# True phase and sizes of PE's instruction blocks in a hand-made list; ut by eight PE transposes; join, nb and y in two pieces

## The chip, the cores and the metric

One core of one Trainium2 chip. The time is device microseconds of one execution of the whole program; the figure is the median of three runs of the kernel.

## The reference

Three parts follow each other: a recurrence over 768 time steps in 32 heads of 40 x 40 state, an MLP of 320 to 2048 to 320, and a gated MLP of 320 to 1536 to 320, both over 3072 tokens.

```python
for t in range(S):                                     # B, H, S, D = 4, 8, 768, 40
    y[:, :, t] = einsum('bhd,bhde->bhe', rt, state)
    Sa = einsum('bhde,bhe->bhd', state, at)
    state = state * wt[:, :, None, :] - einsum('bhd,bhe->bhde', Sa, bt)
    state = state + einsum('bhd,bhe->bhde', vt, kt)
x = y.transpose(0, 2, 1, 3).reshape(B * S, H * D)      # 3072 x 320
h = x @ w_in;  x = (h * sigmoid(1.702 * h)) @ w_out
g = x @ w_gate
return (g * sigmoid(g) * (x @ w_val)) @ w_out2
```

## The kernel before

**Stages.** The recurrence is worked in 12 steps (NT) of 64 time points (T). Step n has two halves: `prepare` (line 637: decay scans, the products nb and nk of the scaled a, b, k, and a triangular solve that gives tt) and `advance` (line 952: w, u, ut, the state update m, the scores sv and su, and the output y, which `give` splits in two and puts into the rows xst of the first MLP). Two steps make one group of 512 tokens for the first MLP (`Up`), whose pieces (`h_part` line 460, `o_part` line 497, eight matmuls each of 512 columns) are called dense here; the attention's matmuls have 32 to 64 columns and are called thin. The gated MLP (`Down`) comes last and is written out by itself.

**The order of the work.** Attention, dense pieces and the weights' conversion are tasks of one `Plan` (line 72). `Plan.order` (line 123) deals them once, when the program is built, into one list; each engine then runs its part of the list in that order, and real waits are kept by semaphores. The dealer keeps a clock of its own: a task has an engine, a cost in us, a due time, and on PE two more things.

- *Density.* Ahead of a thin task it puts up to four dummy matmuls (`warm`, line 435, printed as line 437) until a sum of column work over the last 3.4 us reaches 4000 (lines 199 to 205). It also fills with dummies where PE would sit idle, up to the first dense piece and wherever the dense pieces' one PSUM bank is free (line 195). A dummy writes that bank, from an operand of zeros, `still`.
- *Blocks.* It counts PE instructions (`count`, line 112, 2 to 4 for a matmul with its loads) in `sent`, from 0, and takes it that a block of 256 can't begin earlier than 3.8 us (FETCH) after the one ahead. `cross` adds the missing time to a task, line 185 prefers a dense piece where a thin one would run through a block too fast, and lines 206 to 211 put dummies ahead of a task that would have to wait for a block.

The size of a task in instructions is guessed from its cost: 128 below 1.7 us, 256 below 3 us, 16 for dense pieces and what is shorter than 1.05 us.

**What the change touches.** In `prepare`: `nb_mm` (line 710, 64 matmuls in one task), and in the solve of the first five steps (`pieces`, line 770) `cross_mm` (line 840) and `join_mm` (line 853, 64 matmuls). In `advance`: `u_mm` and its copy `u_out` by ACT into u, a tile of 16 x 40; `ut_mm` (line 1007), which makes u transposed by 32 thin fp32 matmuls (64 matmul records) from w and tt; `m_one` (line 1039), `m_two` (line 1050); the `scores` (line 1151), where ut's halves stand crossed for four of eight heads (`odd`); and `y_one` (line 1115), which in one task adds the old state's part (`y_state`, 32 fp32 matmuls with a drain) and the first half of the new part (`y_part`).

Of the kernel before, what the change touches and what calls it, by code (L numbers as in the profile page):

```python
# [51 lines left out]
class Task:  # L52
    def __init__(self, n, eng, cost, fn, deps, due, bank, kb, same, port):
        self.n, self.fn, self.due, self.deps, self.bank, self.kb, self.same = n, fn, due, deps, bank, kb, same
        self.port = port
        self.choice = dict(zip(eng, cost)) if isinstance(eng, tuple) else {eng: cost}
# [15 lines left out]
class Plan:  # L72
# [5 lines left out]
    BLOCK, FETCH, PACE, AHEAD = 256, 3.8, 0.5, 0.5  # L78
# [9 lines left out]
    def add(self, eng, cost, fn, reads=(), writes=(), due=0.0, after=(), bank=None, kb=0, into=(), same=None, port=True, work=None):  # L88
# [11 lines left out]
        t.work = work  # L100
# [22 lines left out]
    def order(self):  # L123
# [3 lines left out]
        wire = port = hold = began = 0.0  # L127
        sent, pe = 0, []
# [25 lines left out]
        def cross(k, now, cost):  # L154
            nonlocal sent, began
            stop, left = 0.0, self.BLOCK - sent % self.BLOCK
            if k >= left:
                x = now + cost * left / k
                stop = max(0.0, began + self.FETCH - x)
                began = x + stop  # L160
            sent += k
            return stop

        def filler(t, now):
            w = self.fill(t, now)
            w.end += cross(2, now, w.end - now)
# [7 lines left out]
        while True:  # L174
# [17 lines left out]
            if e == "PE":  # L192
# [4 lines left out]
                if t.due < 1e6 and hold < 1e8:  # L197
# [14 lines left out]
                stop = cross(k, now, t.choice[e])  # L212
# [158 lines left out]
class Up:  # L371
# [9 lines left out]
    def __init__(self, tc, ctx, keep, cst, w_out, x2s, side):  # L381
# [13 lines left out]
        self.still = k.tile([128, 128], F32R, name="still")  # L395
# [161 lines left out]
class Attention:  # L557
    EARLY = 5


    def __init__(self, tc, ctx, cst, src, up):
# [21 lines left out]
        self.ut = one.tile([104, 2, H, T], F32, name="ut")  # L583
# [10 lines left out]
        self.u = one.tile([128, 16, D], F32, name="u")  # L594
# [20 lines left out]
        v.memset(self.cend, 1.0)  # L615
        nc.gpsimd.memset(self.mt, 0.0)
# [20 lines left out]
    def prepare(self, plan, n, due):  # L637
# [72 lines left out]
        def nb_mm():  # L710
            ps = self.ps[b.slot]
            x = kb[:, 1]
            for k in range(8):
# [14 lines left out]
        plan.add("PE", 2.4, nb_mm, (ak, "kb1"), ("nb.p",), due + 0.15, bank=b, into=(nbk,), work=1760)  # L728
# [41 lines left out]
        def pieces():  # L770
# [64 lines left out]
            def corners():  # L835
                for i in range(16):
# [16 lines left out]
            def join_mm():  # L853
                ps = self.ps[bt.slot]
                for i, o, c in corners():
# [96 lines left out]
    def advance(self, plan, n, due):  # L952
# [33 lines left out]
        if n:  # L986
            seen = plan.add("PE", 1.2, w_two, (ak, "mt"), ("w.p",), due, bank=bw)
# [12 lines left out]
        def u_out(e):  # L1000
            self.copy(e, self.u.rearrange("q (r k) d -> q r (k d)", r=2), self.ps[bu.slot][:, :, 0:8 * D])
# [19 lines left out]

        def ut_out(e):
            self.copy(e, self.ut.rearrange("q p h t -> q (p h t)"),
# [26 lines left out]
        def m_two():  # L1050
            m_part(1, self.u)
# [18 lines left out]
        if n + 1 < NT:  # L1070
            plan.add("PE", 2.6 if 0 < n < self.EARLY else 1.25, m_one, ("v", "tok0", "mt"), ("m.p",), due + 0.005, bank=bm,
                     work=4300 if 0 < n < self.EARLY else 2200, after=(middle,))
# [6 lines left out]
        plan.add("PE", 1.25, ut_mm, ("w",) + tt, ("ut.p",), due + 0.03, bank=bx, into=("ut",))  # L1079
        plan.add(("ACT",), (1.05,), ut_out, ("ut.p",), ("ut",), due + 0.03, bank=bx)  # L1080

        for src, dst, keys, d in ((self.vt, self.sv, ("vt", "sv"), -0.2), (self.ut, self.su, ("ut", "su"), 0.04)):
            marks = self.scores(plan, src, dst, keys, due + d, src is self.ut)
# [41 lines left out]
        def y_out():  # L1125
# [4 lines left out]
        plan.add("PE", 2.5 if n else 1.25, y_one, ("md", "r", "tok0", "sv"), ("y.p",), due + 0.045, bank=by,  # L1130
                 work=4300 if n else 2500, after=(marks,))
# [19 lines left out]
    def scores(self, plan, src, dst, keys, due, odd):  # L1151
        nc, b = self.nc, self.bank()

        def mm():
            ps = self.ps[b.slot]
            for h in range(H):
                for p in range(2):
                    for z in range(2):
                        d, q = slice(64 * z, 64 * z + D), p ^ h // 4 if odd else p
# [618 lines left out]
```

## Time and profile before

| | |
|---|---|
| median of 3 runs | 1143.59 us (1138.55 to 1144.63) |
| the profiled execution | 1140.57 us, its span 1138.8 us |
| PE busy | 1094.7 us, 96% |
| DVE, ACT, POOL busy | 698.1, 438.1, 108.8 us |
| mean granted clock of PE | 0.978 |

Busy PE time is that of its matmuls, whose ends are modelled; weight loads run beside them and have a row of their own (PEld). [...] A wait that ends on "issue" is one for which the profile shows no other engine and no DMA.

### The profile page before, as it was taken

What the parts mean: (1) busy time and instruction counts of PE and PEld (TensorE: products, weight loads), DVE (VectorE), ACT (ScalarE), POOL (GpSimd) and SP (SyncE); (2) the same over time, 40 slices, a digit from 0 to 9 for tenths busy, and PEclk for the clock granted to TensorE, in tenths of its full rate; (3) what the DMA queues carried; (4) which work ended last, traced back from release to release, by engine and by line L of the source; (5) the groups of instructions that cost most, each with busy time, mean ns of one, the idle gap of its engine ahead of it and who ended that gap; (6) DMA issues with size and microseconds to landing.
All of it is one profiled execution on the core that took longest, in us unless ns stands there. A gap on an engine that the chain in (4) does not pass through costs nothing.

```text
span 1138.8 us, 39991 instructions
## 1 busy us (share of the span) xinstructions
PE 1094.7 (96%) x17403; PEld 908.4 (80%) x17403; DVE 698.1 (61%) x1461; ACT 438.1 (38%) x809; POOL 108.8 (10%) x124
## 2 busy tenths in 40 slices
PE   9888999989999899999999989999999999999987
PEld 7667777767788777877788768788888888888877
DVE  7875788855968687787966166676344344434321
ACT  2434466543434343434335355545222222222221
POOL 1111223301010000000000022221000000000000
PEclk9898999999999999999899999999999999999999
DMA  7245457552534343443423265744233434343000
GB/s 217 88 154 166 149 165 226 159 177 73 180 103 151 112 137 117 134 150 91 145 64 112 83 204 161 218 122 111 75 106 99 129 103 144 93 127 91 24 1 27
DMA packets 141018, 141.99 MB, mean 125 GB/s; under 512 B 16032, under 2 KB 131744, under 8 KB 140832
## 3 DMA queue, kind: packets, MB, share of 16 engines
q1 hardware_dynamic: 134784, 131.48, 38.6%
q10 hardware_dynamic: 6048, 7.86, 2.1%
q8 instruction: 138, 2.26, 0.8%
q14 instruction: 48, 0.39, 0.1%
HBM read 118.04 MB, written 13.11 MB: 115 GB/s over the span
## 4 chain that ended last, share of the span: by engine, by line
PE 84%; DVE 6%; issue 3%; DMA 3%; SPq 2%; ACT 1%; POOL 0%; ACTq 0%; DVEq 0%; POOLq 0%
PE gv L1392 23%; PE h L479 13%; PE sums L511 4%; PE h L437 4%; PE oacc L1413 4%; PE oacc L1412 4%; PE oacc L1411 4%; PE sums L512 3%; PE sums L513 3%; PE ps L1110 2%; PE ps L1034 2%; PE ps L1160 2%; PE sums L507 2%; PE sums L506 2%; PE ps L885 1%
## 5 line engine op out<-in xcount | busy, mean ns | idle before, releaser
L1392 PE MATMUL gv<-xst,wg 128*128 128x512 f32 x1152 | 274.7, 391 | 0.0
L1392 PEld LDWEIGHTS gv<-xst,wg 128*128 128x128 f32 x1152 | 213.8, 188 | 41.3
L479 PE MATMUL h<-xst,wi 120*128 120x512 f32 x768 | 201.8, 405 | 0.4 <-ACT sg L487 0.3
L479 PEld LDWEIGHTS h<-xst,wi 120*128 120x128 f32 x768 | 142.0, 191 | 33.4 <-ACT sg L487 1.6
L1397 DVE TENSOR_TENSOR sg<-gv,sg 128x512 f32<-128x512 f32 x72 | 49.8, 691 | 169.9 <-PE gv L1392 169.2
L487 ACT ACTIVATE sg<-h 128x512 f32<-128x512 f32 x96 | 57.2, 596 | 174.7 <-PE h L479 162.9
L494 DVE TENSOR_TENSOR gl<-sg,gh 128x512 fp32r<-128x512 f32 x82 | 57.5, 701 | 81.7 <-ACT gh L493 81.7
L1398 ACT ACTIVATE gh<-sg 128x512 fp32r<-128x512 f32 x72 | 45.5, 632 | 137.1 <-DVE sg L1397 137.1
L307 POOL TENSOR_TENSOR cvw<-cvu,cva 128x256 uint32<-128x256 uint32 (+2 forms) x89 | 70.9, 798 | 251.1 <-DVE cvu L299 117.9
L1396 ACT ACTIVATE sg<-gv 128x512 f32<-128x512 f32 x72 | 42.9, 596 | 129.1 <-PE gv L1392 128.4
L1413 PE MATMUL oacc<-wo,gl 128*128 128x320 f32 x288 | 89.6, 311 | 0.0
L1412 PE MATMUL oacc<-wo,gh 128*128 128x320 f32 x288 | 89.4, 310 | 0.0
L1411 PE MATMUL oacc<-wo,gh 128*128 128x320 f32 x288 | 89.2, 310 | 0.0
L511 PE MATMUL sums<-gh,wo 128*128 128x512 f32 x192 | 82.0, 427 | 5.8 <-DVE sg L541 4.6
L1399 DVE TENSOR_TENSOR gl<-sg,gh 128x512 fp32r<-128x512 f32 x72 | 49.8, 692 | 50.3 <-ACT gh L1398 50.3
L512 PE MATMUL sums<-gh,wo 128*128 128x512 f32 x192 | 76.5, 399 | 0.0
L513 PE MATMUL sums<-gl,wo 128*128 128x512 f32 x192 | 76.1, 396 | 0.0
L437 PE MATMUL h<-still 128*128 128x512 f32 x232 | 71.4, 456 | 2.0 <-DVE still L396 1.2
L752 DVE TENSOR_TENSOR tsol<-tsol,tmp 128x126 f32<-128x126 f32 (+22 forms) x217 | 58.3, 269 | 6.7
L493 ACT ACTIVATE gh<-sg 128x512 fp32r<-128x512 f32 x96 | 60.7, 632 | 3.5
L744 DVE TENSOR_TENSOR tmp<-tsol,nsol 128x126 f32<-128x126 f32 (+22 forms) x217 | 56.9, 262 | 6.7
L437 PEld LDWEIGHTS h<-still 128*128 128x128 f32 x232 | 47.8, 217 | 12.9 <-DVE still L396 1.2
(176 smaller groups left out, 1652.9 us busy)
## 6 DMA issues: line engine op xcount, KB each, us to landing
wo<-w_out SPq DMA_DIRECT2D x192, 160.0 KB
cva<-out SPq DMA_DIRECT2D x128, 128.0 KB
cva<-gv SPq DMA_DIRECT2D x96, 128.0 KB
kb<-kba SPq DMA_DIRECT2D x92, 104.0 KB
cva<-in_ab SPq DMA_DIRECT2D x64, 120.0 KB
r<-rT SPq DMA_DIRECT2D x48, 104.0 KB
vt<-vT SPq DMA_DIRECT2D x48, 104.0 KB
a<-kba SPq DMA_DIRECT2D x46, 104.0 KB
```

What stands on the lines that cost most here:

```text
L307: nc.gpsimd.tensor_tensor(w.bitcast(U32), u, lo, op=ALU.add)
L437: self.nc.tensor.matmul(self.ph[0].rearrange("q (k c) -> q k c", k=4), c, c.unsqueeze(1).to_broadcast([128, 4, 128]), start=True, stop=True)
L479: nc.tensor.matmul(ps[:, 0:n], self.wi[:, b, 128 * f:128 * f + 128], x[:, a], start=(e == 0), stop=(e == 7))
L493: add("ACT", 0.63, lambda: nc.scalar.activation(out=hi, in_=sg, func=ACTF.Copy), (f"sg{s}",), (f"gh{d}",))
L511: nc.tensor.matmul(acc[k], w[:, c:c + 128], hi, start=st, stop=False)
L512: nc.tensor.matmul(acc[k], w[:, 256 + c:384 + c], hi, start=False, stop=False)
L513: nc.tensor.matmul(acc[k], w[:, c:c + 128], lo, start=False, stop=sp)
L752: self.engine(e).tensor_tensor(t, t, self.tmp[:, 0:(16 - o) * u].rearrange("q (c i) -> q c i", c=16 - o), op=ALU.add)
L1392: nc.tensor.matmul(ps, w[:, b], x[:, a], start=(i == 0), stop=(i == 7))
L1411: nc.tensor.matmul(acc[k], hi[:, c], self.wo[:, f, 0], start=st, stop=False)
L1412: nc.tensor.matmul(acc[k], hi[:, c], self.wo[:, f, 1], start=False, stop=False)
L1413: nc.tensor.matmul(acc[k], lo[:, c], self.wo[:, f, 0], start=False, stop=sp)
```

## The change

- The dealer's block count starts at 63 (HEAD), and tasks may say their size in instructions: nb 256, cross 261, the merged m_one 137, the second half of w and the old part of y 129; ut falls to 16. A dense piece still counts 16.
- A block is taken to need 3.4 us instead of 3.8, and the time that is left in it is reckoned from the matmuls' bare durations (`real`, `least`) plus half (SURE) of what else passed, no longer from the time passed alone.
- nb of step zero (HALVES = 1) and join of the first five steps (EARLY) become two tasks each; the old state's part of y becomes a task `y_old` of its own from step 1 on.
- ut is made from u by eight transposes of 128 x 128 (u is widened to 16 x 64, zeroed once on POOL), laid out by head first, so `odd` goes.
- The dummy's operand `still` becomes one column that is read with step zero, for the weights and for the 512 columns.
- The flag at the end of attention is worked in columns of the tile `good` instead of a tile of its own.

```diff
-    BLOCK, FETCH, PACE, AHEAD = 256, 3.8, 0.5, 0.5
+    BLOCK, FETCH, PACE, AHEAD, HEAD, SURE = 256, 3.4, 0.5, 0.5, 63, 0.5
...
+        return t.size or (16 if t.due >= 1e6 or t.choice["PE"] < 1.05 else 128)
+
+    def least(self, t):
+
         c = t.choice["PE"]
-        return 16 if t.due >= 1e6 or c < 1.05 else 128 if c < 1.7 else 256 if c < 3 else 384
+        return t.real or (1.87 if t.due >= 1e6 else min(c, 1.15))
...
-        sent, pe = 0, []
+        wire = port = hold = began = lean = 0.0
+        sent, pe = self.HEAD, []
...
+        def spare(x, y):
+            return began + self.FETCH - x if self.SURE >= 1.0 else self.FETCH - y - self.SURE * max(0.0, x - began - y)
+
+        def cross(k, now, cost, real):
+            nonlocal sent, began, lean
+            stop, part = 0.0, k
+            left = self.BLOCK - sent % self.BLOCK
+            while part >= left:
+                x = now + stop + cost * (k - part + left) / k
+                y = lean + real * left / k
+                stay = max(0.0, spare(x, y))
+                stop += stay
+                began, lean = x + stay, 0.0
+                sent, part, left = sent + left, part - left, self.BLOCK
+            sent += part
+            lean += real * part / k
             return stop
...
-                if t.due < 1e6 and (sent % size + k) / size * self.FETCH > now + t.choice[e] - began + self.PACE:
+                if t.due < 1e6 and (sent % size + k) / size * self.FETCH - self.PACE > self.FETCH - spare(
+                    now + t.choice[e], lean + self.least(t)
+                ):
...
-                            x = began + self.FETCH - now - t.choice[e] * left / k
+                            x = spare(now + t.choice[e] * left / k, lean + self.least(t) * left / k)
...
-        self.still = k.tile([128, 128], F32R, name="still")
+        self.still = k.tile([128, 1], F32R, name="still")
...
-            self.ph[0].rearrange("q (k c) -> q k c", k=4), c, c.unsqueeze(1).to_broadcast([128, 4, 128]), start=True, stop=True
+            self.ph[0], c.to_broadcast([128, 128]), c.to_broadcast([128, 512]), start=True, stop=True
...
+        if n < self.HALVES:
+            for j in (0, 4):
+                plan.add("PE", 1.2, lambda j=j: nb_mm(j, j + 4), (ak, "kb1"), ("nb.p",), due + 0.15, bank=b, into=(nbk,),
+                         work=880, real=0.72)
+        else:
+            plan.add("PE", 2.4, lambda: nb_mm(0, 8), (ak, "kb1"), ("nb.p",), due + 0.15, bank=b, into=(nbk,), work=1760,
+                     size=256, real=1.44)
...
+                for i, o, c in corners(8 * j, 8 * j + 8):
...
-            plan.add("PE", 2.7, cross_mm, ("xa", "dd"), ("x.p",), due + 0.1, bank=bx, into=("q0", "q1"), work=2900)
+            plan.add("PE", 2.7, cross_mm, ("xa", "dd"), ("x.p",), due + 0.1, bank=bx, into=("q0", "q1"), work=2900,
+                     size=261, real=2.5)
...
-            plan.add("PE", 2.3, join_mm, ("tn", "q0", "q1"), ("tt.p",), due + 0.1, bank=bt, into=("tt0", "tt1"), work=1280)
+            for j in range(2):
+                plan.add("PE", 1.15, lambda j=j: join_mm(j), ("tn", "q0", "q1"), ("tt.p",), due + 0.1, bank=bt,
+                         into=("tt0", "tt1"), work=640, real=0.64)
...
-            w = self.w.rearrange("q i d -> q (i d)")
             for h in range(H):
-                for p in range(2):
-                    for z in range(2):
-                        r, g = divmod(h, 4)
-                        i = 8 * r + 2 * g + z
-                        q, m = p ^ r, D if z else 64
-                        s = slice(64 * q, 64 * q + 64)
-                        nc.tensor.matmul(
-                            ps[64 * z:64 * z + m, q, T * h:T * h + T], w[s, D * i:D * i + m], self.tt[s, i],
-                            start=True, stop=True,
-                        )
+                nc.tensor.transpose(
+                    ps[:, h // 4, 128 * (h % 4):128 * (h % 4) + 128], self.u[:, 2 * h:2 * h + 2].rearrange("q z d -> q (z d)"), self.ident
+                )
...
+                     size=137 if 0 < n < self.EARLY else 128, real=2.5 if 0 < n < self.EARLY else 1.1)
...
-        plan.add("PE", 1.25, ut_mm, ("w",) + tt, ("ut.p",), due + 0.03, bank=bx, into=("ut",))
+        plan.add("PE", 0.9, ut_mm, ("u",), ("ut.p",), due + 0.03, bank=bx, into=("ut",))
...
+        def y_old():
+            y_state(1)
+            nc.tensor.drain()
+            y_state(0)
+
         def y_one():
-            if n:
-                y_state(1)
-                nc.tensor.drain()
-                y_state(0)
...
-        plan.add("PE", 2.5 if n else 1.25, y_one, ("md", "r", "tok0", "sv"), ("y.p",), due + 0.045, bank=by,
-                 work=4300 if n else 2500, after=(marks,))
+        if n:
+            plan.add("PE", 1.25, y_old, ("md", "r"), ("y.p",), due + 0.045, bank=by, work=2200, after=(marks,), size=129)
+        plan.add("PE", 1.25, y_one, ("tok0", "sv"), ("y.p",), due + 0.045, bank=by, work=2100, after=(marks,))
```

## Rows read from the trace of the kernel before

**Rows 1.** The page, part 1: busy us, share of the span, instructions.

```profile
PE 1094.7 (96%) x17403; PEld 908.4 (80%) x17403; DVE 698.1 (61%) x1461; ACT 438.1 (38%) x809; POOL 108.8 (10%) x124
```

**Rows 2.** Windows: busy us per engine (PE, PEld, DVE, ACT, POOL), clock, DMA.

```profile
0.00:138.00 138.00, 125.07 (x3304) 98.46 (x3304) 105.71 (x215) 52.62 (x104) 24.65 (x35) 0.91 0.51 154
138.00:645.00 507.00, 489.34 (x11713) 394.75 (x11713) 367.73 (x803) 220.36 (x383) 49.63 (x45) 0.99 0.44 132
...
735.00:1138.80 403.80, 394.71 (x2034) 346.83 (x2032) 169.46 (x325) 114.80 (x212) 13.43 (x18) 0.99 0.30 90
```

**Rows 3.** Windows of line 437 alone, the dummy: PE, PEld, clock, DMA.

```profile
0.00:138.00 138.00, 67.92 (x221) 45.99 (x221) 0.91 0.51 154
```

**Rows 4.** PE's waits, 0 to 138 us: total us, times, longest; seven "issue" rows.

```profile
PE ps L848 <- issue: 2.9, 1, 2.9
...
PE ps L1034 <- issue: 0.3, 1, 0.3
```

**Rows 5.** PE's waits, 138 to 645 us; eight "issue" rows.

```profile
PE ps L1110 <- issue: 3.3, 3, 2.4
...
PE ps L1034 <- issue: 0.2, 1, 0.2
```

**Rows 6.** Timeline of PE, 88 to 92 us: start, us, line, tiles, count, idle before.

```profile
88.53 0.21 PE L1160 MATMUL sums<-r,vt 40*64 40x64 f32 x1 [0.47 <-issue]
88.67 1.20 PE L885 MATMUL ps<-tt,nb 32*32 32x32 f32 x64
89.80 1.14 PE L965 MATMUL ps<-v,nk 64*64 64x40 f32 x63
92.15 0.25 PE L965 MATMUL ps<-v,nk 64*64 64x40 f32 x1 [1.21 <-issue]
```

**Rows 7.** Timeline of PE: the first and the last of eleven long stalls.

```profile
49.50 1.00 PE L885 MATMUL ps<-tt,nb 32*32 32x32 f32 x50 [1.16 <-issue]
...
434.10 0.40 PE L511 MATMUL sums<-gh,wo 128*128 128x512 f32 x1 [1.17 <-issue]
```

**Rows 8.** Timeline of PE around 385 us: y_one and the dense piece behind it.

```profile
384.99 0.87 PE L1110 MATMUL ps<-sv,tok 64*64 64x64 f32 x45 [2.40 <-issue]
385.79 3.58 PE L479 MATMUL h<-xst,wi 120*128 120x512 f32 x8
```

**Rows 9.** Timeline of PE, 578 to 597 us: m_two, ut_mm, and eight transposes of mt.

```profile
578.32 1.13 PE L1034 MATMUL ps<-u,tok 64*64 64x40 f32 x64
...
581.42 1.16 PE L1017 MATMUL ps<-tt,w 64*64 64x64 f32 x64
582.51 0.97 PE L437 MATMUL h<-still 128*128 128x512 f32 x3
...
595.40 0.92 PE L1140 MATMUL ps<-cst,mt 104*104 104x104 f32 x8
596.10 1.17 PE L479 MATMUL h<-xst,wi 120*128 120x512 f32 x4
```

**Rows 10.** Timeline of PE, 229 to 235 us: cross_mm and the tokens behind it.

```profile
229.14 1.35 PE L848 MATMUL ps<-nsol,tsol 32*16 32x32 f32 x128
...
234.23 0.96 PE L941 MATMUL ps<-cst,kb 104*128 104x104 f32 x9 [2.96 <-issue]
```

**Rows 11.** Windows of 4 us, all engines, behind three stalls and behind eight transposes.

```profile
52.00:56.00 4.00, 4.00 (x70) 3.00 (x70) 3.66 (x12) 2.18 (x6) 0.73 (x1) 0.50 0.29 96
...
246.00:250.00 4.00, 4.00 (x71) 2.94 (x69) 0.00 (x0) 2.25 (x4) 0.00 (x0) 0.57 0.78 244
386.00:390.00 4.00, 4.00 (x50) 2.77 (x53) 0.77 (x4) 0.59 (x1) 0.00 (x0) 0.57 0.14 46
...
595.00:599.00 4.00, 4.00 (x60) 3.53 (x50) 3.66 (x11) 1.14 (x2) 0.00 (x0) 1.00 0.13 43
```

**Rows 12.** Timeline of PE at 681 us: the start of a group's sums.

```profile
681.36 0.80 PE L511 MATMUL sums<-gh,wo 128*128 128x512 f32 x1 [4.05 <-DVE sg L541]
```

**Rows 13.** Groups of instructions by line: u's copy by ACT; busy, mean ns, idle.

```profile
L627 ACT ACTIVATE u<-ps 128x640 f32<-128x640 f32 x11 | 7.6, 693 | 8.2 <-PE ps L996 8.2
```

More of the change, by code (lines that the diff above doesn't have):

```diff
@@ L55, in __init__ @@
         self.port = port
+        self.work = self.size = self.real = None
         self.choice = dict(zip(eng, cost)) if isinstance(eng, tuple) else {eng: cost}
@@ L86, in __init__, with add @@
         self.sets = sets
-    def add(self, eng, cost, fn, reads=(), writes=(), due=0.0, after=(), bank=None, kb=0, into=(), same=None, port=True, work=None):
+    def add(self, eng, cost, fn, reads=(), writes=(), due=0.0, after=(), bank=None, kb=0, into=(), same=None, port=True, work=None,
+            size=None, real=None):
         deps = {d for d in after if d}
@@ L99, in add @@
         t = Task(len(self.tasks), eng, cost, fn, deps, due, bank, kb, same, port)
-        t.work = work
+        t.work, t.size, t.real = work, size, real
         for d in deps:
@@ L152, in start @@
             return s
[L154 to L161, printed above, removed]
+        def spare(x, y):
[13 more added lines that the diff above has]
+            lean += real * part / k
             return stop
@@ L165, in filler @@
             w = self.fill(t, now)
-            w.end += cross(2, now, w.end - now)
+            w.end += cross(2, now, w.end - now, 0.23)
             done.append(w)
@@ L557 @@
 class Attention:
-    EARLY = 5
+    EARLY, HALVES = 5, 1
     def __init__(self, tc, ctx, cst, src, up):
@@ L582, in __init__ @@
         self.vt = one.tile([104, 2, H, T], F32, name="vt")
-        self.ut = one.tile([104, 2, H, T], F32, name="ut")
+        self.utr = one.tile([104, H, 2, T], F32, name="ut")
+        self.ut = self.utr.rearrange("q h p t -> q p h t")
         self.tok = [one.tile([128, 16, D], F32, name=f"tok{i}") for i in range(2)]
@@ L593, in __init__ @@
         self.w = one.tile([128, 16, D], F32, name="w")
-        self.u = one.tile([128, 16, D], F32, name="u")
+        self.u = one.tile([128, 16, T], F32, name="u")
         self.sv = one.tile([128, 2, H, T], F32, name="sv")
@@ L615, in __init__ @@
         v.memset(self.cend, 1.0)
+        nc.gpsimd.memset(self.u, 0.0)
         nc.gpsimd.memset(self.mt, 0.0)
@@ L708, in prepare, with nb_mm @@
         b = self.bank()
-        def nb_mm():
+        def nb_mm(k0, k1):
             ps = self.ps[b.slot]
             x = kb[:, 1]
-            for k in range(8):
+            for k in range(k0, k1):
                 for h in range(2):
@@ L833, in pieces, with corners @@
             bx, bt = self.bank(), self.bank()
-            def corners():
-                for i in range(16):
+            def corners(i0=0, i1=16):
+                for i in range(i0, i1):
                     for c in range(0, 128, 32):
@@ L851, in cross_mm, with join_mm @@
                     )
-            def join_mm():
+            def join_mm(j):
                 ps = self.ps[bt.slot]
-                for i, o, c in corners():
+                for i, o, c in corners(8 * j, 8 * j + 8):
                     nc.tensor.matmul(ps[o, 0, c], self.tn[o, i], self.q[o, i], start=True, stop=True)
@@ L986, in advance @@
         if n:
-            seen = plan.add("PE", 1.2, w_two, (ak, "mt"), ("w.p",), due, bank=bw)
+            seen = plan.add("PE", 1.2, w_two, (ak, "mt"), ("w.p",), due, bank=bw, size=129)
         plan.add(("ACT",), (0.74,), w_out, ("w.p",), ("w",), due, bank=bw)
@@ L1000, in u_out @@
         def u_out(e):
-            self.copy(e, self.u.rearrange("q (r k) d -> q r (k d)", r=2), self.ps[bu.slot][:, :, 0:8 * D])
+            self.copy(e, self.u.rearrange("q (r k) d -> q r k d", r=2)[:, :, :, 0:D],
+                      self.ps[bu.slot][:, :, 0:8 * D].rearrange("q r (k d) -> q r k d", d=D))
         tt = ("ttl", "tt0", "tt0.0", "tt1")
@@ L1071, in advance @@
             plan.add("PE", 2.6 if 0 < n < self.EARLY else 1.25, m_one, ("v", "tok0", "mt"), ("m.p",), due + 0.005, bank=bm,
-                     work=4300 if 0 < n < self.EARLY else 2200, after=(middle,))
+                     work=4300 if 0 < n < self.EARLY else 2200, after=(middle,),
+                     size=137 if 0 < n < self.EARLY else 128, real=2.5 if 0 < n < self.EARLY else 1.1)
             plan.add("PE", 1.25, m_two, ("u", "tok1"), ("m.p",), due + 0.02, bank=bm, work=2200)
@@ L1215, in give, with att_flag @@
         plan.add("NONE", 0.001, lambda: None, tuple(f"xq{i}" for i in range(4)), (key,), due)
-def att_flag(nc, tc, att, good):
-    with tc.tile_pool(name="fl", bufs=1) as p:
-        m = p.tile([104, 2], F32, name="fl_m")
-        nc.vector.tensor_reduce(
-            out=m[:, 0:1], in_=att.cend.rearrange("p h x -> p (h x)"), axis=AXL.X, op=ALU.min
-        )
-        nc.vector.tensor_reduce(out=m[:, 1:2], in_=att.over, axis=AXL.X, op=ALU.max)
-        nc.vector.tensor_scalar(out=m[:, 0:1], in0=m[:, 0:1], scalar1=CMIN, scalar2=None, op0=ALU.is_ge)
-        nc.vector.tensor_scalar(out=m[:, 1:2], in0=m[:, 1:2], scalar1=0.0, scalar2=None, op0=ALU.is_le)
-        nc.vector.tensor_tensor(good[0:104], m[:, 0:1], m[:, 1:2], op=ALU.mult)
+def att_flag(nc, att, good):
+    m = good[0:104, 1:3]
+    nc.vector.tensor_reduce(out=m[:, 0:1], in_=att.cend.rearrange("p h x -> p (h x)"), axis=AXL.X, op=ALU.min)
+    nc.vector.tensor_reduce(out=m[:, 1:2], in_=att.over, axis=AXL.X, op=ALU.max)
+    nc.vector.tensor_scalar(out=m[:, 0:1], in0=m[:, 0:1], scalar1=CMIN, scalar2=None, op0=ALU.is_ge)
+    nc.vector.tensor_scalar(out=m[:, 1:2], in0=m[:, 1:2], scalar1=0.0, scalar2=None, op0=ALU.is_le)
+    nc.vector.tensor_tensor(good[0:104, 0:1], m[:, 0:1], m[:, 1:2], op=ALU.mult)
 def bad_flag(nc, tc, down, cst, least, good, bad):
```

22 lines of the change are left out of this document (10 added, 12 removed).

## The prediction

> **What bounds the kernel now.** I read the page first: PE is busy for 1094.7 of 1138.8 us, 96% [rows 1]. So the time is PE's work, PE's gaps, and the time that PE runs at the lower of its two clock levels. Then I cut the span where the kind of work changes [rows 2]. Until 138 us there is no dense work of the first layer; PE has attention steps 0, 1 and a part of 2, and fills its waits with the dummy matmul of line 437: 221 of them, 67.92 us, 0.31 us each [rows 3]. From 138 to 645 us attention is dealt into the dense work and PE is busy for 489.34 of 507 us. The rest of the first layer follows without attention, and from 735 us the second layer, which the change doesn't touch. The granted clock is 0.91 in the first stretch, 0.99 in the second [rows 2].
>
> Next I asked what PE waited for in the two stretches. In the first, seven rows of waits end on "issue", from 2.9 us down to 0.3: 8.8 us together [rows 4]. In the second, eight such rows, from 3.3 down to 0.2, sum to 9.9 of the 17.7 us of idle time [rows 5]; the other rows there are waits on DVE and ACT. "Issue" means that nothing in the profile held PE back. One row after another shows what it is: between the stalls at 88.53 and 92.15 us stand 1 + 64 + 63 matmuls, each with a weight load, so 256 instructions [rows 6]. I counted loads, matmuls, drains and semaphore instructions from the stall at 49.50 to the one at 434.10, the first and last of the eleven that are over 0.8 us at the weight load: 18,945, which is 74 x 256 + 1, and the nine between them fall on the same grid within two instructions [rows 7]. So PE receives its program in blocks of 256, and stops where the next one is late. The first boundary lies 194 instructions after PE's first, so some 62 or 63 went ahead of the list: that is the 63 of the diff. The list of before starts its count at 0 and counts 256 for a merged m_one that is 137 long: it keeps blocks apart at places where none ends.
>
> [...]
>
> **The change part by part.**
>
> *Transposed u.* The 64 matmuls (with 64 loads) of ut_mm hold PE from 581.42 to 582.51, 1.09 us. Eight transposes of 104 columns hold it from 595.40 to 596.10, 0.70 us [rows 9]. The new ones have 128 columns: 0.70 x 128/104 = 0.86 us (bounds 0.70 and 1.09). That is 0.23 us less, in nine steps after 138 us: **-2 us** (bounds -3.5 and 0). Before 138 us a dummy takes the place. The added wait is on u's copy out of PSUM by ACT. It costs nothing as long as the second half of m goes first, which reads the same u: it stood at 578.32, three us ahead of ut_mm [rows 9]. Behind ut_mm on PE stand dense work and the next step; ACT's ut copy keeps its size. If the cover were gone, the price is a wait of about that copy, 0.69 us a step [rows 13]. It also takes 112 instructions out of each step (128 become 16), nearly half a block.
>
> *True blocks, after 138 us.* A stall here is lost whole, since dense work was ready. The longest stand where 256 thin instructions ran in one piece: inside y_one, 2.40 us at 384.99 [rows 8], and in the token transposes behind cross_mm, 2.96 us at 234.23 [rows 10]. y_one is cut in two (129 and 128), join in two of 128, so a dense piece of 2 us can stand between; cross_mm stays whole at 261. What can't go: the new list counts on 3.4 us for a block, while the stalled blocks took 3.62 us [rows 6] and, by the grid, about 5 (cross_mm's matmuls start at 229.14, by the grid within 0.1 us of a boundary, and the next block came at 234.23) [rows 10]. I let 3 of the 9.9 us stay: **-7 us** (bounds -9.9 and 0).
>
> *Clock behind the stalls.* After two of these stalls the granted clock is 0.57 over 4 us [rows 11], which is the lower level for 3.4 us, so 4 x 0.43 = 1.7 us of work lost each; the dense piece behind 384.99 took 3.58 us [rows 8]. **-3 us** (bounds -3.4 and, if new gaps bring as many new ones, +3.4).
>
> *Before 138 us.* A stall here is no gain by itself: the block still has to come, and the list now puts dummies there. What they can save is the clock. At 0.91 the stretch lost 0.09 x 138 = 12.4 us of PE's work [rows 2], much of it right behind the seven stalls (0.50 over 52 to 56 us, behind the one at 49.50) [rows 7, 11], and dummies and attention stand in one queue, so a slow dummy delays what is behind it. I take a quarter back, -3 us. The cuts go the other way: each new piece (join in steps 0 to 2, nb in step 0, y in steps 1 and 2: six more) is checked by itself against the list's wish for density and may draw up to four dummies, 0.31 us each [rows 3]. Most stand where density was there already; I take +1. Stretch: **-2 us** (bounds -10: the clock and dummies put at wrong boundaries; +7: 6 x 4 x 0.31).
>
> *At nothing.* The one-column dummy operand reads zeros as before and keeps its 512 columns; no row shows a one-column read, the nearest is the dummy itself, and I take its 0.31 us. The memset of u stands on POOL at the program's start, beside those of mt and md, ahead of all data. The flag edits only move where six tiny DVE results lie. No DMA is added; but the whole list is dealt anew, so SP's and ACT's queues get another order, which is the main uncertainty. One place where that shows is at 681 us, where PE waits 4.05 us for a chain on ACT and DVE [rows 12]; it may go or grow, and I leave it.
>
> Sum: -2 - 7 - 3 - 2 = -14 us. The profiled execution took 1140.57 us (span 1138.8 and 1.8 around it), 3 us under the median of 1143.59 and near the middle of the three runs. 1140.57 - 14 = 1126.6; since the median lies higher, I say **1128 us**, 1.4% below it. What is next late is DVE and ACT: their part of PE's 17.7 us stays.
>
> **The rivals.**
>
> *The stalls move instead of going.* For it: blocks that stalled took 3.62 us and more, against 3.4 in the new list (3.8 before), and the spare time is discounted by half of the waits. Against: the eight rows stand for ten waits in some ninety blocks after 138 us [rows 5]. Then only ut and the clock's small change are left: 1140.6 - 2 - 2 = 1137 us, 1133 to 1143 with the median's lean.
>
> *Slower: dummies in the first stage.* Place: PE before the first dense matmul, steps 0 to 2. Price: six pieces with four dummies, 7 us, and two more slow-clock stretches of 1.7 us, with neither -7 nor -3 behind it because the dealt list is no better: 1140.6 + 7 + 3.4 = 1151 us. It decides once the first dense matmul of the first layer starts after about 146 us (138 now, and 8 us more eat what the rest gives up to the clock).
>
> *The fetch is hidden anyway.* If other causes hold PE at those boundaries, only ut is left: 1138.5 us. The grid of 256 [rows 6, 7] speaks against. [...]
>
> *Transposes slow the clock.* If eight transposes in a row let the granted clock fall, each of nine steps loses 1.7 us: 1140.6 - 14 + 15 = 1142 us. Against: eight of them stand at 595.40 and the clock over 595 to 599 is 1.00 [rows 9, 11]. [...]
>
> **How the numbers follow.** Forecast 0.62 (1114 to 1136); stalls move 0.20 (1133 to 1143); slower 0.10 (1145 to 1158); fetch hidden 0.04; transposes 0.04. A measurement of this kernel tells about 0.5% from no change, so faster is below 1137.9 and slower above 1149.3. Faster: 0.60 of the forecast, half of the second, a part of the fourth: 0.70. Slower: 0.08. Same: 0.22. The range is 1112 to 1144: from the first stage at its best (8 us more) with the 3 us of stalls and the 4.05 us [rows 12] gone too, to the upper end of the first rival.
>
> **What would show it.** Right: PE's "issue" rows after 138 us sum to 4 us or less; ut_mm is eight records of about 0.86 us together; no 4 us stretch between 138 and 640 at 0.57 behind an "issue" stall; the first dense matmul at 130 to 138 us. Wrong: "issue" waits that stay near 10 us at other lines; more than 221 dummies before the first dense matmul, or this one after 146 us; new waits of PE on ACT's u copy.

## The result, and the profile after

| | before | after |
|---|---|---|
| median of the runs | 1143.83 us (1138.55 to 1145.18) | 1129.34 us (1124.95 to 1136.78) |
| ratio of the times | | 0.9889, interval 0.9849 to 0.9930 |
| the profiled execution, its span | 1140.57, 1138.8 us | 1127.17, 1125.4 us |
| first dense piece starts at | 137.94 us | 128.73 us |
| from there to the first gv matmul | 597.0 us | 587.1 us |
| second layer (first gv to the end) | 403.9 us | 409.6 us |

The change made the kernel 1.1% faster: 1129.3 us against a forecast of 1128, a saving of 13.4 us in the profiled executions against a sum of 14. The stages say at once that the total came out better than its parts: the first stage gave 9.2 us (forecast 2), the rest of the first layer 9.9 (forecast 12), and the second layer, taken as untouched, cost 5.7.

The page, part 1 (busy us, share of the span, instructions), answers [rows 1]:

```profile
PE 1083.7 (96%) x16716; PEld 900.9 (80%) x16716; DVE 698.1 (62%) x1467; ACT 436.8 (39%) x809; POOL 99.2 (9%) x119
```

Windows by stage, columns as in [rows 2]:

```profile
0.00:128.70 128.70, 112.97 (x3036) 91.27 (x3036) 100.91 (x204) 49.91 (x99) 22.91 (x30) 0.91 0.51 152
128.70:616.40 487.70, 473.81 (x11235) 384.43 (x11233) 368.75 (x815) 216.69 (x380) 42.24 (x45) 0.99 0.46 138
715.80:1125.40 409.60, 400.67 (x2034) 347.19 (x2032) 163.35 (x308) 110.56 (x200) 9.46 (x12) 0.99 0.28 85
```

The window of the first stage for line 453 alone, the dummy, as in [rows 3]:

```profile
0.00:128.70 128.70, 54.94 (x194) 38.56 (x194) 0.91 0.51 152
```

The first stage holds 194 dummies of 54.94 us where it had 221 of 67.92: 13 us of dummy time left a stage that became 9.2 us shorter. Its mean clock is 0.91, as before.

PE's waits between the first dense piece and the end of attention (total us, times, longest), which answer [rows 5]:

```profile
PE ps L992 <- ACT q L645: 1.9, 1, 1.9
PE sums L527 <- DVE sg L557: 1.7, 2, 1.1
PE h L453 <- ACT sg L503: 1.5, 1, 1.5
PE ps L880 <- issue: 1.4, 1, 1.4
PE h L495 <- issue: 1.4, 1, 1.4
PE ps L738 <- issue: 1.3, 1, 1.3
...
PE ps L1054 <- issue: 0.5, 1, 0.5
```

"Issue" is 4.6 us here where it was 9.9 [rows 5]. The long ones inside y and in the token transposes [rows 8, 10] are gone; the longest left is 1.4 us. Counted as in the prediction (loads, matmuls, drains and semaphore instructions, PE's first as 0), all thirteen "issue" waits of the changed kernel stand 192 or 193 instructions behind a multiple of 256. So do 228 of the 231 in the fourteen profiles of this document; the other three last less than 0.2 us each. The pages have an instruction queue whose packets fit such blocks (packets, MB, share of 16 engines), before and after:

```profile
q8 instruction: 138, 2.26, 0.8%
```

```profile
q8 instruction: 133, 2.18, 0.8%
```

Both are 16.4 KB a packet, and PE's loads and matmuls together are 252 a packet before and 251 after.

### The profile page after: what moved, and what is told of

Its sections match the earlier page's. It is cut to its first block, busy times and chain, and to the rows that moved or that the text cites. A ratio compares the mean times of both kernels' runs of the same rounds, so it can differ in the third digit from the quotient of the medians.

```text
span 1125.4 us, 38617 instructions
## 1 busy us (share of the span) xinstructions
PE 1083.7 (96%) x16716; PEld 900.9 (80%) x16716; DVE 698.1 (62%) x1467; ACT 436.8 (39%) x809; POOL 99.2 (9%) x119
## 4 chain that ended last, share of the span: by engine, by line
PE 86%; DVE 6%; DMA 4%; issue 2%; ACT 1%; SPq 1%; ACTq 0%; DVEq 0%
PE gv L1412 24%; PE h L495 14%; PE sums L527 4%; PE oacc L1433 4%; PE oacc L1432 4%; PE oacc L1431 4%; PE sums L528 3%; PE sums L529 3%; PE h L453 3%; PE ps L1183 2%; PE ps L1054 2%; PE ps L1131 2%; PE sums L523 2%; PE sums L522 2%; PE ps L738 1%
## 5 line engine op out<-in xcount | busy, mean ns | idle before, releaser
L1412 PE MATMUL gv<-xst,wg 128*128 128x512 f32 x1152 | 280.7, 396 | 0.0
L510 DVE TENSOR_TENSOR gl<-sg,gh 128x512 fp32r<-128x512 f32 x85 | 60.4, 711 | 77.4 <-ACT gh L509 77.3
L527 PE MATMUL sums<-gh,wo 128*128 128x512 f32 x192 | 80.7, 420 | 3.8 <-DVE sg L557 3.8
L1419 DVE TENSOR_TENSOR gl<-sg,gh 128x512 fp32r<-128x512 f32 x72 | 49.8, 692 | 50.2 <-ACT gh L1418 50.2
L528 PE MATMUL sums<-gh,wo 128*128 128x512 f32 x192 | 75.4, 393 | 0.0
L453 PE MATMUL h<-still 128*128 128x512 f32 x217 | 61.5, 427 | 2.8 <-ACT sg L503 1.5
L776 DVE TENSOR_TENSOR tsol<-tsol,tmp 128x126 f32<-128x126 f32 (+22 forms) x217 | 55.3, 255 | 6.6
L1432 PEld LDWEIGHTS oacc<-wo,gh 128*128 128x128 f32 x288 | 54.3, 189 | 3.2
```

Source lines behind the costliest of these rows:

```text
L453: self.nc.tensor.matmul(self.ph[0], c.to_broadcast([128, 128]), c.to_broadcast([128, 512]), start=True, stop=True)
L510: add(("DVE", "POOL"), (0.74, 1.35), lambda e: self.engine(e).tensor_tensor(lo, sg, hi.bitcast(F32), op=ALU.subtract), (f"sg{s}", f"gh{d}" ...
L527: nc.tensor.matmul(acc[k], w[:, c:c + 128], hi, start=st, stop=False)
L528: nc.tensor.matmul(acc[k], w[:, 256 + c:384 + c], hi, start=False, stop=False)
L1412: nc.tensor.matmul(ps, w[:, b], x[:, a], start=(i == 0), stop=(i == 7))
L1432: nc.tensor.matmul(acc[k], hi[:, c], self.wo[:, f, 1], start=False, stop=False)
```

## The experiments

Stage lengths are read from the timeline: from the first matmul of line 495 (a dense piece) to the end of the last y matmul, and from the first gv matmul to the end. The first run is the kernel before once more, the second the changed kernel once more, on the chip that ran the next two. The granted clock is a share of full speed; 1.00 is the highest and 0.50 the lowest mean of the windows [rows 11]. Work lost to the clock is reckoned as in the prediction: the length of a stretch times what its mean granted clock lacks to 1.

> The kernel before, unchanged, on the chip of the next three. The second layer's stage (from its first gv matmul to the end) took 403.9 us in the profile of before and 409.6 us in that of after, with one gv matmul every 227 and every 232 ns at a granted clock of 1.00 in both, though the change doesn't touch that stage. If this is the place of the tile wg in memory, this run shows 227 ns and 403 to 405 us whatever the chip; if it is the chip or the execution, it shows the value of the other kernels of this call.

> The changed kernel, unchanged. Place theory: one gv matmul every 232 ns and a second-layer stage of 409 to 411 us, again. Execution theory: the same pace as the kernel before has in this call. Time 1125 to 1137 us either way; the granted clock's low stretches (18.8 us lost of PE's work in the first profile) should differ little, since the order of the work is fixed.

Before: 1144.48 us (one run; the ratio is against eleven of it on that chip), first dense piece at 141.98 us. After: 1131.05 us (1129.02 to 1133.26), ratio 0.9865 (0.9817 to 0.9912), first dense piece at 130.38 us, issue waits of 4.0 us behind it. The gain repeats, and so does the longer second layer: 404.3 us of before against 408.5.

### Where wg lies

The second layer does the same 1152 gv matmuls in both kernels, but their steps grew from 227 to 232 ns. What moved is the weights' tile: `still`, shrunk from 512 bytes of each partition to 4, lies ahead of it, and wg went from byte 58336 to 57856. The edit puts an empty tile in between, which also moves back the two tiles behind wg in its pool, wo2 and xr. The gv matmuls read wg and xst, and xst lies ahead of all of these:

```diff
+        self.pad = wp.tile([128, 120], F32, name="pad")
+        self.nc.vector.memset(self.pad[:, 0:1], 0.0)
         self.wg = wp.tile([128, NF2, 2, 6, 128], F32R, name="wg")
```

> The changed kernel with 480 bytes of padding ahead of the second layer's weights, which puts wg, wo2 and xr back to the addresses they had before (wg at 58336 instead of 57856 bytes of each partition). Place theory: one gv matmul every 227 ns, second-layer stage 403 to 405 us, the whole 5 to 6 us faster than the changed kernel (1121 to 1126 us). Execution theory: no difference to the changed kernel in this call.

The gv group by lines (busy us, mean ns of one, idle before): the kernel before, the changed kernel, and the changed kernel with the tile back.

```profile
L1392 PE MATMUL gv<-xst,wg 128*128 128x512 f32 x1152 | 274.7, 391 | 0.0
```

```profile
L1412 PE MATMUL gv<-xst,wg 128*128 128x512 f32 x1152 | 280.7, 396 | 0.0
```

```profile
L1414 PE MATMUL gv<-xst,wg 128*128 128x512 f32 x1152 | 274.9, 391 | 0.0
```

With the old place the second layer takes 403.8 us: the 6 us are back, at the same order of work and the same mean clock of 0.99. All fourteen profiles agree: the five kernels with the wide `still` or the empty tile take 227 ns a step, the nine with neither take 232. Why the place matters is not shown. The whole time was 1130.0 us (1122.22 to 1138.12), ratio 0.9839 (0.9796 to 0.9882): the whole did not come to the 1121 to 1126 us expected, and the 6 us drown in what the earlier stages do from one execution to the next. The profiled one had its first dense piece at 136.30 us with the same list that gave 128.73 and 130.38.

### The count of blocks, told wrong and made wrong

Two ways to break the true count. The first tells the dealer a wrong phase, so that it deals another list:

```diff
-    BLOCK, FETCH, PACE, AHEAD, HEAD, SURE = 256, 3.4, 0.5, 0.5, 63, 0.5
+    BLOCK, FETCH, PACE, AHEAD, HEAD, SURE = 256, 3.4, 0.5, 0.5, 191, 0.5
```

> The changed kernel, whose list starts its count of PE instructions at 191 instead of 63: the true sizes stay, but every boundary that the list keeps in mind lies half a block (128 instructions) away from a real one. Theory of the true phase: the waits on issue in the dealt stretch come back from 4.6 to about 10 us, with the clock's low stretches behind them, and the time is 6 to 12 us above the changed kernel. Rival (the gain is the finer cut and fewer instructions, the phase doesn't matter): within 3 us of the changed kernel.

It took 1164.62 us (1156.51 to 1175.45), ratio 1.0139 (1.0090 to 1.0188), but not for the reason expected. PE's waits from the first dense piece to the end of attention:

```profile
PE sums L527 <- DVE sg L557: 6.1, 1, 6.1
PE ps L912 <- DVE nk L954: 4.8, 2, 4.6
...
PE ps L1054 <- issue: 2.9, 2, 2.3
```

and the longest of the second layer:

```profile
PE gv L1412 <- DMA wg<-wg: 8.4, 2, 8.0
```

All issue rows of that stretch sum to 4.6 us, no more than in the changed kernel. The new list waits on DVE and ACT, and in the second layer for the weights. Up to the first gv matmul it waits 21.8 us on DVE and ACT (the changed kernel 9.7) and loses 15.4 us to the lower clock (5.1). So a newly dealt list can be 30 us worse for reasons that have nothing to do with blocks, and a comparison across two lists can't price the count.

The second way keeps the list and moves the blocks, by 128 instructions ahead of it:

```diff
+    c = up.still
+    for i in range(76):
+        up.nc.tensor.matmul(up.ph[0][:, 0:2], c.to_broadcast([128, 128]), c.to_broadcast([128, 2]), start=True, stop=True)
+    skip = 12
     for t in order:
+        if skip and t.fn == plan.warm:
+            skip -= 1
-        if t.begin <= end:
+        elif t.begin <= end:
             t.run()
```

> The changed kernel with its list untouched, but TensorE gets 128 instructions more before the list (76 two-column multiplications of the zero tile in, the first 12 dummies out, so that the start takes about as long). Every one of TensorE's blocks of 256 instructions now ends half a block away from where the list was dealt for. Theory (the dealer's true count of blocks is what took the stalls away): laid over the times of the changed kernel's own instructions, blocks shifted by 128 would be shorter than 3.5 us by 5.2 us in all before the first dense piece (unshifted 1.2) and by 7.7 us between it and the end of attention (unshifted 0.1). So the waits put down to issue rise from 7.7 and 4.6 us to about 12 and 12, two or three clock drops come back behind them, and the run is 9 to 16 us longer than the kernel with 256 instructions more (about 1140 to 1147 beside 1131). Rival (the count is beside the point, the gain is the five shorter steps and ut): issue waits within 2 us of the unshifted, time within 3 us of it.

> The control of the kernel with 128 instructions more: 256 more (152 two-column multiplications in, the first 24 dummies out), so every block ends where it did in the changed kernel's list, one block later in number. Both theories: the changed kernel's time, 1129 to 1134, issue waits about 8 and 4.5 us. If it were slower by 5 us or more, what comes ahead of the list would cost by itself, and the half block could not be read.

(The whole block: 152 of them, 24 dummies out.) Half a block: 1143.1 us (1134.74 to 1146.38), ratio 0.9956 (0.9925 to 0.9988). Whole block: 1155.53 us (1151.42 to 1161.98), ratio 1.0090 (1.0058 to 1.0122). The control is the slower one, so the totals can't be read; the timeline of the half block's kernel shows why:

```profile
1.05 16.37 PE L1288 MATMUL h<-still 128*128 128x2 f32 x76 [1.05 <-DVE still L412]
17.28 10.04 PE L453 MATMUL h<-still 128*128 128x512 f32 x31
27.25 0.82 PE L738 MATMUL ps<-kb,a 40*32 40x32 f32 x64
```

A two-column multiplication with 128 by 128 weights took 215 ns, so the first nb stood at 27.25 us instead of 15.12 (at 40.81 with 152 of them). The same edits with 32 by 32 zeros cost less: 64 of them and no dummy out (half block), and 152 of them with 24 dummies out (whole block, with wg at its old place besides). For these:

> The changed kernel with its list untouched and 128 instructions ahead of it again, this time 64 multiplications of 32 by 32 zeros, because two-column ones cost 215 ns each. By the nb rows of the changed kernel (64 multiplications of this form in 1.15 us) they take 1 to 4 us and lie in the 2.7 us in which TensorE waits for kb, so the first nb starts at 15 to 17 us. Theory (the true count matters for this list): issue waits about 9 to 12 us before the first dense piece and 8 to 10 us behind it (7.7 and 4.6 unshifted), the time from first dense piece to the end of attention 494 to 500 us (unshifted 488 to 491), the time 5 to 12 us above that of the kernel with the long start, which has the same closed gap and the true blocks. Rival (the count is beside the point): within 3 us of it.

> The changed kernel's list untouched, 256 instructions more ahead of it (152 multiplications of 32 by 32 zeros in, the first 24 of the 43 dummies out), so that every block ends where the list was dealt for, and TensorE is busy until about 15 us: 152 at the 56 ns that they took in the half block kernel is 8.5 us, 19 dummies some 5 to 7 us. And wg lies at byte 58336 again, as in the kernel before. It is the counterpart of the half block kernel of 32 by 32 zeros and an attempt at a faster version. Theory: clock 1.00 over 15 to 29 us and the first dense piece at 121 to 126 us as in the half block kernel (123.2), the stretch from it to the end of attention 486 to 491 us (half block 493.5 and 495.0) with 3.5 to 5 us of issue waits (6.9 and 7.9), the stage from the first gv on 404 us (without the place 408.5 to 410.3): span 1112 to 1120, ratio to before 0.975 to 0.982. Rival (the closed gap only moves the clock's fall to later in the first stage, as with the long start and the whole nb): first dense piece at 128 to 133 us, ratio 0.983 to 0.988.

PE's issue waits behind the first dense piece with half a block more:

```profile
PE ps L1054 <- issue: 2.4, 2, 2.1
PE ps L738 <- issue: 1.2, 1, 1.2
PE ps L912 <- issue: 0.8, 1, 0.8
PE ps L1131 <- issue: 0.7, 1, 0.7
...
PE ps L921 <- issue: 0.5, 1, 0.5
PE h L495 <- issue: 0.5, 2, 0.4
PE ps L1023 <- issue: 0.5, 1, 0.5
...
PE ps L1183 <- issue: 0.4, 1, 0.4
```

and with a whole block more:

```profile
PE ps L738 <- issue: 1.2, 1, 1.2
PE ps L992 <- issue: 1.2, 1, 1.2
PE ps L1023 <- issue: 1.1, 1, 1.1
...
PE ps L880 <- issue: 0.9, 1, 0.9
PE ps L1054 <- issue: 0.5, 1, 0.5
PE ps L921 <- issue: 0.4, 1, 0.4
```

| the changed kernel's list, dense start to end of attention | issue waits, us | length, us |
|---|---|---|
| blocks where the list expects them (after, its repeat, old place, whole block two-column and 32 by 32) | 4.6, 4.0, 5.4, 3.7, 5.3 | 487.6, 488.8, 495.0, 490.7, 489.7 |
| half a block off (two-column, 32 by 32) | 8.0, 7.0 | 495.0, 493.5 |

Half a block off costs some 3 us of stalls, less than the 3.4 to 7.4 expected, and the lengths overlap, since the clock's falls differ by as much between executions (up to the first gv the changed kernel lost 5.1 us of work to them, with wg at its old place 10.2). With the work lost to the clock taken off they no longer do: 482.5 to 486.4 us where the blocks fit, 488.2 and 491.0 half a block off. Ahead of the first dense piece the shift raised no stalls, though 9 to 12 us were expected: 6.7 us of issue waits in both kernels of 32 by 32 zeros, 9.6 (half) and 10.3 (whole) in the two-column ones. In the whole it can't be seen, and the half block was to be 5 to 12 us slower than the long start (below) and was 8 us faster: 1128.16 us (1124.07 to 1136.35), ratio 0.9872 (0.9825 to 0.9918), against 1128.24 us (1125.56 to 1132.46), 0.9846 (0.9818 to 0.9874), for the whole block, which also has the 6 us of wg's place. That place is there again: 404.0 us for its second layer.

### The steps alone, the dealer alone

The first kernel has the changed steps (ut, join, nb, y) and the dealer of before. The second has the steps of before and the changed dealer with their true sizes:

```diff
-        plan.add("PE", 2.3, join_mm, ("tn", "q0", "q1"), ("tt.p",), due + 0.1, bank=bt, into=("tt0", "tt1"), work=1280)
+        plan.add("PE", 2.3, join_mm, ("tn", "q0", "q1"), ("tt.p",), due + 0.1, bank=bt, into=("tt0", "tt1"), work=1280, size=256, real=1.28)
...
-                 work=4300 if n else 2500, after=(marks,))
+                 work=4300 if n else 2500, after=(marks,),
+                 size=257 if n else None, real=2.3 if n else None)
```

> The changed kernel's steps (ut by eight transposes, join and the first nb in two parts, y in two) dealt by the dealer of before (block count from 0, sizes guessed from the estimated time, 3.8 us for a block). Theory: the stalls stay where the dealer does not know the blocks: issue waits about 9 to 11 us in each of the two stretches, time 1139 to 1146 less nothing but ut's 2 us and plus the later stage's 6 us: ratio to before 0.995 to 1.005. Rival (shorter steps cannot run through a block, and that is the gain): issue waits after the first dense piece 5 us or less, ratio 0.985 to 0.992.

> The kernel before with the changed kernel's dealer alone: block count from 63, true sizes for its undivided steps (nb 256, join 256, cross 261, y 257, the rest as in the change), 3.4 us for a block. Theory: most of the gain: issue waits after the first dense piece 4 to 6 us (before 9.9), the long steps keep one stall each here and there, ut stays at 1.09 us; ratio 0.988 to 0.995. Rival (the divided steps are what matters): issue waits 8 us or more, ratio 0.997 to 1.004. The list is dealt anew in this kernel and in the one with the steps alone, so either may be off by some us for waits that have nothing to do with blocks.

Steps alone: 1138.04 us (1129.16 to 1146.31), ratio 0.9916 (0.9878 to 0.9954). Dealer alone: 1154.81 us (1153.36 to 1159.82), ratio 1.0088 (1.0055 to 1.0122). In both the rival had the mechanism right, and the dealer alone was slower than either theory allowed. The longest wait and all the issue waits behind the first dense piece, for the steps alone:

```profile
PE ps L898 <- DVE nk L940: 6.6, 5, 4.1
...
PE ps L898 <- issue: 1.1, 1, 1.1
...
PE ps L866 <- issue: 0.4, 1, 0.4
PE h L481 <- issue: 0.4, 1, 0.4
PE ps L724 <- issue: 0.3, 1, 0.3
```

and the larger waits of that stage and the rest of the first layer for the dealer alone:

```profile
PE sums L526 <- DVE sg L556: 6.1, 4, 2.1
PE h L494 <- ACT sg L502: 5.5, 5, 2.5
PE ps L957 <- ACT md L642: 4.1, 1, 4.1
PE ps L735 <- issue: 2.7, 2, 1.4
PE sums L522 <- issue: 2.4, 1, 2.4
```

With the shorter steps 2.2 us of issue waits are left, though that dealer counts from 0 and guesses sizes. But its list waits on DVE and ACT instead, 16.1 us up to the first gv matmul (before 9.2), so PE's idle time there is 18.3 us, hardly less than before (19.1); the changed kernel has 14.3. It also has the narrow `still` and, with 2.0 us of waiting for the weights, a second layer of 413.5 us. With the true count alone 8.8 us stay. Its list starts dense work at 127.35 us, 10 us earlier than before, and then takes 620.4 us to the first gv (before 597.0): its waits on DVE and ACT sum to 22.5 us there, in before to 9.2 and in its repeat to 10.8. It keeps the wide `still` and has a second layer of 404.3 us. These are new lists again, so they don't say what either part is worth on the changed kernel's list.

### The start

The changed list puts 43 dummies ahead of the first half of nb, where before 47 stood ahead of the whole. PE runs out of them; timeline:

```profile
1.05 11.36 PE L453 MATMUL h<-still 128*128 128x512 f32 x43 [1.05 <-DVE still L412]
15.12 1.15 PE L738 MATMUL ps<-kb,a 40*32 40x32 f32 x64 [2.71 <-DVE kb L712]
```

The window 15 to 29 us:

```profile
15.00:29.00 14.00, 13.88 (x325) 11.42 (x329) 6.65 (x19) 5.47 (x10) 0.00 (x0) 0.52 0.68 209
```

Behind a 2.71 us wait the granted clock is 0.52 over these 14 us: 0.48 x 14 = 6.7 us of work. In the kernel before that window has 1.00. Two kernels close the gap (0.94 us of it stay in the second), one with the last 11 of the 43 dummies in fp32 (`up.still.bitcast(F32)` as both operands), one with nb whole again:

```diff
-    EARLY, HALVES = 5, 1
+    EARLY, HALVES = 5, 0
```

> The changed kernel with its list and its number of instructions untouched, but the last 11 of the 43 dummies at the start multiply in plain fp32, some 0.5 us each instead of 0.22, so TensorE is busy until kb has come at about 15 us. In the changed kernel it waits 2.3 to 3.1 us there and its clock lies at half from 15 to 29 us. Theory (cutting the first nb took four dummies from ahead of it, and the gap drops the clock): no wait for kb, clock 1.00 over 15 to 29 us, the first dense piece 3 to 6.8 us earlier (122 to 127 instead of 128.7 to 130.4), ratio to before 0.980 to 0.985. Rival (the other engines set the pace of the first stage): first dense piece within 1.5 us of the changed kernel's, ratio 0.986 to 0.990.

> The changed kernel with nb of step zero undivided (one step of 256 instructions); the list differs in its first 142 lines only, and 47 dummies stand ahead of nb, as in the kernel before, instead of 43. Theory: as with the long start, no gap ahead of nb, clock 1.00 over 15 to 29 us, the first dense piece 3 to 6.8 us earlier, ratio 0.980 to 0.985. Rival (the undivided nb runs through a block and stands for the fetch): a stall of about 1 us within it and the later part as before, ratio 0.986 to 0.990.

Long start: 1136.14 us (1130.73 to 1140.72), ratio 0.9939 (0.9909 to 0.9969). Whole nb: 1131.2 us (1127.84 to 1135.45), ratio 0.9892 (0.9853 to 0.9932). Clock over 15 to 29 us is 1.00 in both, and still the first dense piece came at 136.48 and 132.90 us. The windows show what happened, in the long start over 81 to 101 us, in the whole nb over 34 to 41 and 78 to 85:

```profile
81.00:101.00 20.00, 19.53 (x427) 15.43 (x434) 9.74 (x19) 8.91 (x19) 6.45 (x6) 0.50 0.59 177
```

```profile
34.00:41.00 7.00, 6.73 (x139) 4.66 (x140) 6.90 (x9) 0.70 (x1) 0.00 (x0) 0.53 0.06 16
78.00:85.00 7.00, 5.05 (x138) 4.09 (x139) 4.84 (x10) 4.27 (x11) 2.11 (x3) 0.51 0.54 154
```

The clock fell later instead. The long start also ran over: its 11 fp32 dummies are 22 matmul records of 9.65 us together, 0.88 us a dummy where 0.5 was expected, so nb came at 19.98 us and the ends of the blocks moved too. The whole block of 32 by 32 zeros closed the gap as well (first nb at 15.46 us) and then had 0.51 over 74 to 98 us and its first dense piece at 131.65 us, where its rival had it; the half block, with first nb at 16.20, was the one that gained: 123.23 us, with 4.3 us of work lost to the clock in the first stage where the changed kernel lost 12.0. Without that loss its first stage is no shorter (118.9 us against 116.8). One execution each; that closing the gap is worth anything is not shown.

## Why the prediction came out right, and where its steps did not

**Transposed u (-2).** Right. Timeline of a late step:

```profile
603.07 1.04 PE L1038 MATMUL ps<-cst,u 128*128 128x128 f32 x8
603.86 2.08 PE L495 MATMUL h<-xst,wi 120*128 120x512 f32 x8
```

The next instruction starts 0.79 us behind it, 0.85 in most other steps, against 1.08 for the 64 records: ten steps behind the first dense piece (I had counted nine) at 0.23 us are 2.3 us. PE's only wait on ACT's ut copy is one of 0.3 us, in the first stage. The rival of a slower clock is out: the window 602.5 to 606.5 us, behind these eight, has 1.00, and so have the 4 us from the start of each of the other nine.

**Stalls (-7).** 9.9 became 4.6: -5.3. The size is a little off, as I let 3 stay. The reason given was half wrong: I credited the true count and the shorter steps together. The runs divide them in part. The shorter steps take the stalls away with either dealer (2.2 and 4.6 us left); the true count alone takes next to none (8.8 left). But with the old dealer other waits took the stalls' place; only steps and dealer together brought PE's idle time down. On the list that was dealt for it, the count is worth some 3 us of stalls behind the first dense piece.

**Clock behind the stalls (-3).** Right in sign, and smaller. Between the first dense piece and the first gv, the work lost to the lower clock, summed from the granted clock over that stretch, fell from 10.2 to 5.1 us; but of that only 1.7 us is of falls at issue stalls (two before, at 244.79 and 384.99 us; one after). The rest is of falls behind waits on DVE and ACT, such as the one of 4.05 us [rows 12], which I had left alone. Nor is it steady: the repeats lost 6.8 and 5.1 us, and the changed list with wg at its old place 10.2. The forecast that no stretch at 0.57 would stand behind an issue stall failed once (236 to 240 us at 0.58, behind 1.41 us at 236.91). The longest one left, 182 to 189 us, stands behind a wait on ACT of 1.94 us at 180.86.

**Before 138 us (-2).** Wrong in size: -9.2. I priced a stall there at nothing and took the clock as the only gain. But the clock took 12.0 us of work in both; what went is dummies, 13 us of them. I had priced only dummies that the cuts might add, while the list needed fewer. Both parts have a share, as the dealt lists go: the steps alone start dense work at 128.74 us and the dealer alone at 127.35. Nor is it steady: one list gave 128.73, 130.38 and 136.30 us. There the clock does count: without the work lost to it (12.0, 12.0 and 18.8 us) the three are 116.8, 118.4 and 117.5 us. Reckoned so, the kernel before has 126.0 and 128.3, the steps alone 118.5 and the dealer alone 122.2: the shorter stage is the list's, and the steps bring most of it.

**At nothing.** This is where the sum missed a cost. The one-column `still` moved wg: 5.7 us in a stage that I took as untouched. I had looked at what the smaller operand does where it is read, not at the tiles laid out behind it. The four dummies that the cut of nb took from the start belong here too; the clock's fall behind their gap took 6.7 us of work, though no gain from closing it is shown.

So -2.3 - 5.3 - 5.1 - 9.2 + 5.7 is -16.2; +2.8 is left for what I did not list; 12 more dummies behind the first dense piece than before (23 against 11, 6.6 us against 3.5) are about that, though nothing shows that they are the cause. The total was met by luck: the first stage gave 7 us more than I allowed and the second layer took 6. Three of the signs that I had named were just missed: issue waits of 4 us or less (4.6, in the repeat 4.0), the first dense matmul at 130 to 138 us (128.73), and no stretch at 0.57 behind an issue stall (one).

**The rivals.** Stalls that only move (1137) and the slower first stage (1151) did not come: 4.6 us of issue waits, 128.73 us. The hidden fetch (1138.5) fell with the half block: with nothing but the blocks' phase changed, issue waits rose from between 3.7 and 5.4 us to 7.0 and 8.0, and they stand on the same grid of 256 in the program, so at other steps of the list.

The attempt at a faster version, a whole block of zeros and wg at its old place, gave 0.9846 (0.9818 to 0.9874), the changed kernel 0.9889 and, in its repeat, 0.9865; the intervals overlap, and the gain of the place is shown for its stage alone.

## What to carry to other kernels

Where thin matmuls ran through whole blocks of 256 instructions, the stalls went with shorter steps, between which a long matmul can stand (9.9 us became 2.2 with the steps alone); counting the blocks exactly was worth less (some 3 us on the list dealt for it). But read PE's whole idle time and not the stalls alone: the list with 2.2 us of stalls still left PE idle for 18.3 us up to the first gv, against 19.1 before. When a tile is resized, read the stages that use the tiles behind it, even those that no edit touches: here one took 5.7 us more. Take the work lost to the clock off a stage before comparing two executions of it: 128.73, 130.38 and 136.30 us of one list became 116.8, 118.4 and 117.5. And don't price one rule of a dealer by dealing again: keep the list and move the one thing.

## What was not expected of the hardware

- All "issue" waits of PE of 0.2 us or more, in the profile of every kernel of this document, stand 192 or 193 instructions behind a multiple of 256, also where 128 instructions more were put ahead of the same list.
- The pace of the 512-column gv matmuls went with the place of their weights' tile: 227 ns a step with wg at byte 58336 of the partition, 232 ns at 57856, both at clock 1.00.
- A two-column matmul with 128 by 128 weights took 215 ns (76 in 16.37 us; its load 333 ns, overlapped), one of 32 by 32 some 56 ns (64 in 3.59 us), at clock 1.00.
- The 11 plain fp32 dummies of 512 columns in the long start are 22 matmuls in the records, 9.65 us together.
